# Phase 2 by token tiles of one batch with one stacked low-rank product; queries beside the chunks turned by VectorE

## The chip, the cores and the metric

The kernel runs on one core of one Trainium2 chip. The metric is the device time of one execution in microseconds (us). Before the change three executions took 1484.17, 1484.77 and 1485.76 us, so the median is 1484.77 us. The execution that the profiler recorded took 1491.34 us, and its first to last instruction spans 1489.6 us.

## The reference, cut to what matters

All arrays are float32, batch 8, 8 heads, 576 tokens, head size 64, model size 512.

```python
# attention through 32 packed queries per head
p_packed = sm_attn(p, k, v)              # (8, 8, 32, 64)
x = sm_attn(q, p_packed, p_packed)       # (8, 8, 576, 64) -> (8, 576, 512)
# first mixer (phase 1)
xk = mu_k * x + (1 - mu_k) * x_prev;  xr = mu_r * x + (1 - mu_r) * x_prev
x = sigmoid(xr @ w_r) * (relu(xk @ w_k) ** 2 @ w_v)
# second mixer (phase 2)
h = x.transpose(0, 2, 1) @ U @ V         # U (576, 32), V (32, 576): over the tokens
u = x + h.transpose(0, 2, 1)
out = u + relu(u @ w_ch1) @ w_ch2        # 512 -> 2048 -> 512
```

## The kernel before, in words

**Order of the work.** `Plan` collects every operation with its reads and writes, and `emit` lays the operations out on the engines with a list scheduler: it knows a cost for each operation, takes the ready operation of the lowest class first, on PE and SP in the order of the program and on the others in the order of becoming ready, and so fixes one instruction order for each engine and for SP's queue of DMA issues. On the chip each engine runs its list in order; an instruction that waits holds all behind it.

**Attention.** A unit is one pair of batches and one pair of heads; there are 16. Units 0 to 7 (`plain`) run ahead of everything else in several lanes. Units 8 to 15 run in one lane, A0, beside the chunks of phase 1; they are not plain. `attention_steps` (L648) does one unit: it turns k by TensorE, scores the packed queries, takes a softmax, turns q, forms the packed values `pp`, scores q against them and writes the result to `x_d`. For q it loads `qin` (`load_q`, L621): two DMAs, one for each batch, the tokens of the two batches in alternating partitions, runs of 64 floats. Then nine 128x128 transposes on TensorE, three into each PSUM bank (L718 to L731), and three copies of 384 columns, by ScalarE or VectorE, move the result to `qt`. In a unit of the lane A0 the next unit's q is loaded one unit ahead, as soon as its buffer is free: eight buffers of the pool `big` go round, eight to a unit. The scores for units 8 to 15 are turned back by VectorE (`turn`, L825 and L831).

**Phase 1** works on 12 chunks of 384 columns (`chunks`, three for each pair of batches); a column tile of 128 holds 64 tokens of each of the two batches. `mix` makes xk and xr, `r_block`, `k_block` and `v_block` do the three products with every fp32 operand split in a high and a low fp32r part, three products each (`PASS`). `x2_out` writes the rows of token tile i to `x2_d`, and `xu_block` sums x times U over the tokens and writes it to `xu_d` for each pair b of batches: rows for high and low part, batch and rank.

**Phase 2** works on 36 token tiles T of 128 tokens, nine for each pair of batches, four to a group q (`NQ` = 9). Tile T holds tokens 9p+i of both batches, 64 partitions each. `load_u` (L1252) loads it with one DMA. `h_block` (L1260) adds the low-rank term: two matmuls of 128x512 accumulate in one bank, with `vst` (the high part of V, then the low part, zero where the batch is the other one) as the stationary operand and `X` of the pair as the moving one; VectorE adds the bank to the tile. `load_xu` (L1240) makes `X` from four DMAs, one sum, one copy and one subtraction. `t_block` turns the tile for the next products, `operands` and `product` (L1319) run a seven-product scheme for u @ w_ch1, `c2_block` (L1342) multiplies by w_ch2 and, at a group's end, adds u and stores each tile by one DMA. The weights of `product` are streamed by DMAs that GpSimd issues (L319, `wb<-ws_d`). For each group the preparation of the next one (loads, `h_block`, `t_block`, `operands`) is spread over the eight steps f (L1487).

Of the kernel before, what the change touches and what calls it, by code (L numbers as in the profile page):

```python
# [9 lines left out]
F32 = mybir.dt.float32  # L10
F32R = mybir.dt.float32r
# [466 lines left out]
def packed_attention_moe_mixer_kernel(  # L478
# [36 lines left out]
    NPLAIN = 8  # L515
# [4 lines left out]
    plan = Plan(nc)  # L520
    add, sub, mul = ALU.add, ALU.subtract, ALU.mult
# [15 lines left out]
    x2_d = [dtile(f"x2_d{b}", [P, NI * DM], tuple(range(NI))) for b in range(NBP)]  # L537
    xu_d = [dtile(f"xu_d{b}", [P, DM]) for b in range(NBP)]
# [38 lines left out]
    class Bufs:  # L577
# [22 lines left out]
            return self.kept[1:]  # L600

        def tile_in(self, tag):
            return plan.tile(self.big_p, [P, 1152], F32, "big", parts=(0, 1, 2, 3), name=tag)

        def load_k(self, u, after=()):
            bp, j = divmod(u, NJ)
# [14 lines left out]
        def load_q(self, u, after=()):  # L621
            bp, j = divmod(u, NJ)
            if u not in self.qin:
                self.qin[u] = self.tile_in("qin")
            t = self.qin[u]
            for b2 in range(2):
                plan.dma(
                    t.at(b2)[b2:P:2, :].rearrange("p (i h d) -> p i h d", i=NI, h=2),
                    q[2 * bp + b2, 2 * j:2 * j + 2].rearrange("h (p i) d -> p i h d", i=NI), after=after)
# [18 lines left out]
    def attention_steps(A, u, u_next):  # L648
        bp, j = divmod(u, NJ)
        kin, qin, vin = A.kin.pop(u), A.qin.pop(u), A.vin.pop(u)  # L650
# [15 lines left out]
        for b2 in range(2):  # L666
            yield
            ps = ps_att()
# [5 lines left out]
        ps = ps_att()  # L674
# [36 lines left out]
        for b2 in range(2):  # L711
            r = slice(b2 * 64, (b2 + 1) * 64)
# [2 lines left out]
        plan.reduce(s0[:, 8:9], s1[:, 4:8], add)  # L715
        plan.recip(s0[:, 9:10], s0[:, 8:9])

        for c in range(3):  # L718
            yield
            ps = ps_att()  # L720
            for t in range(3):
                i = 3 * c + t
                plan.transpose(ps[:, t * P:(t + 1) * P], qin[:, i * P:(i + 1) * P], ident)
            n = 3 if c < 2 or not plain else 2
            w = 8 if plain else NI
            plan.copy(
                qt[:, 0:w * P].rearrange("p (b i c) -> p i b c", b=2, i=w)[:, 3 * c:3 * c + n],
                ps[:, 0:n * P].rearrange("p (i c b) -> p i b c", i=n, b=2))
            if c == 2 and plain:
# [11 lines left out]
        ps = ps_att()  # L741
# [4 lines left out]
        ps = ps_att()  # L746
        for t in range(5):
            for g in range(4):
# [4 lines left out]
                        start=(t == 0), stop=(t == 4), skip_group_check=True)  # L753
# [3 lines left out]
        if not plain:  # L757
            for b2 in range(2):
                r = slice(b2 * 64, (b2 + 1) * 64)
# [5 lines left out]
        ps = ps_att()  # L765
# [13 lines left out]
        if plain:  # L779
# [15 lines left out]
            for g, src, g0, g1 in ((0, psa, 0, 16), (1, psb[:, 0:P], 16, 20)):  # L795
                sv = src.rearrange("p (g k) -> p g k", k=NP)
# [8 lines left out]
            ps = ps_att()  # L805
# [4 lines left out]
            ps = ps_att()  # L810
# [4 lines left out]
        else:  # L815
            n = S // NP
# [371 lines left out]
    vst_ = []  # L1188

    def make_v():  # L1190
        vst = plan.tile(vx_p, [P, 2, NI, 2, 64], F32R, "vst", parts=(0, 1))
        vst_.append(vst)
        for c in range(2):
            raw = plan.tile(st_p, [P, 512], F32, "s", parts=(0, 1, 2, 3), name="raw_v")
            for g in range(4):
                plan.dma(raw.at(g)[g * 32:(g + 1) * 32, 0:288], v_d[:, c * 288:(c + 1) * 288])
            for i0, i1 in ((0, 5), (5, NI)):
                s = plan.tile(st_p, [P, 512], F32, "s", name="s_v")
                sv = s[:, 0:(i1 - i0) * 64].rearrange("p (i b c) -> p i b c", b=2, c=32)
                plan.zero(sv)  # L1200
                for g in range(4):
                    gr = slice(g * 32, (g + 1) * 32)
                    plan.copy(sv[gr, :, g % 2, :],
                              raw[gr, 0:288].rearrange("p (c i) -> p i c", i=NI)[:, i0:i1], ("dve",))
                sl = slice(c * 32, (c + 1) * 32)
                split(vst.at(0)[:, 0, i0:i1, :, sl], vst.at(1)[:, 1, i0:i1, :, sl], sv)

    def make_ws(f):
        r = []
# [28 lines left out]
        w2[m] = b  # L1238

    def load_xu(b):  # L1240
        xa = plan.tile(st_p, [P, 512], F32, "s", parts=(0, 1), name="xa")
        xb = plan.tile(st_p, [P, 512], F32, "s", parts=(0, 1), name="xb")
# [3 lines left out]
        plan.tt(xa[:, 0:512], xa[:, 0:512], xb[:, 0:512], add)  # L1246
        X = plan.tile(vx_p, [P, 512], F32R, "X")
        plan.copy(X, xa[:, 0:512])
        plan.tt(X[64:128, :], xa[64:128, 0:512], X[64:128, :], sub)
        xt[b] = X  # L1250

    def load_u(T):  # L1252
        b, i = divmod(T, NI)
        pl, tag = (((u_p, "u"),) * 4 + ((r_p, "r"),) * 3 + ((x2_p, "x2"),) * 3)[T % 10]
        u_t[T] = plan.tile(pl, [P, DM], F32, tag, name="u")
        plan.dma(u_t[T], x2_d[b].at(i)[:, i * DM:(i + 1) * DM])

    prep_banks = [ps_a]

    def h_block(T):  # L1260
        b, i = divmod(T, NI)
# [80 lines left out]
    def c2_block(q, m, th, h, last):  # L1342
        if (q, th) not in first:
            first.add((q, th))
            acc[q, th] = [plan.bank(ps_c2, "psc2") for _ in range(2)]
            fresh = True
        else:
            fresh = False
        w = w2[m]
        for t in range(2):  # L1350
            for i, (a, wi) in enumerate(PASS):
                plan.mm(acc[q, th][t], half(h, a)[:, t * P:(t + 1) * P], half(w, wi),
                        start=(fresh and i == 0), stop=(last and i == 2))
        if last:
            for t in range(2):
                T = 4 * q + 2 * th + t
                b, i = divmod(T, NI)
# [209 lines left out]
```

## Time and profile before

| | |
|---|---|
| median of three executions | 1484.77 us |
| profiled execution | 1491.34 us, span 1489.6 us |
| PE (TensorE matmul) busy | 1461.4 us, 98% of the span |
| PEld (weight load) | 1277.7 us, 86% |
| DVE (VectorE) | 980.2 us, 66% |
| ACT (ScalarE) | 728.3 us, 49% |
| POOL (GpSimd) | 270.3 us, 18% |
| mean granted TensorE clock | 0.983 of full speed |

Busy shares are means over stages with different limits, so each stage has to be read by itself. Up to about 130 us the first eight attention units run alone; then come the chunks of phase 1, up to about 520 us with attention beside them; from about 730 us it is phase 2. Matmuls are pipelined: the duration of one matmul is longer than its pitch, the time from its start to the start of the next, and the price of one in a full queue is the pitch. A line such as L197 is that of a helper that records every matmul, so groups are told apart by their tiles: `psat` is attention, `psk`, `psv`, `psr` are phase 1, `psh` is the low-rank term, `psc` the products of phase 2.

### The profile page before, as it was taken

How to read it: one execution, taken by the hardware profiler on the slowest of the kernel's cores; microseconds unless marked ns; L12 is line 12 of the kernel's file. 1: busy time of each engine (PE TensorE's matmuls, PEld its weight loads, DVE VectorE, ACT ScalarE, POOL GpSimd, SP SyncE). 2: the span in 40 equal slices, each digit the busy share in tenths (PEclk: the TensorE clock that was granted, in tenths of full speed). 3: DMA queues.
4: the chain of work that ended last, by engine and by line, in shares of the span. 5: the costliest groups of instructions: out<-in, count | busy, mean ns of one | idle time of the engine just before them, and what ended most of it. 6: DMA issues, size and time to landing. Idle time of an engine off the chain costs nothing.

```text
span 1489.6 us, 25587 instructions
## 1 busy us (share of the span) xinstructions
PE 1461.4 (98%) x9208; PEld 1277.7 (86%) x9208; DVE 980.2 (66%) x2143; ACT 728.3 (49%) x1534; POOL 270.3 (18%) x522
## 2 busy tenths in 40 slices
PE   6999999999999999999999999999999999999998
PEld 5667888888888888889899999899999999999997
DVE  6677877788888888786855464545555555554533
ACT  5567656666666666676533233323333332333332
POOL 0000000000000000001333333333333333333331
PEclk9689999999999999999999999999999999999999
DMA  8863335654655446666988888888888878878763
GB/s 233 234 175 121 114 101 137 205 182 136 186 179 156 141 141 218 207 226 191 314 228 237 211 208 245 198 244 229 231 212 229 213 201 239 213 216 222 206 176 99
DMA packets 213708, 292.42 MB, mean 196 GB/s; under 512 B 70224, under 2 KB 105360, under 8 KB 213584
## 3 DMA queue, kind: packets, MB, share of 16 engines
q1 hardware_dynamic: 141008, 158.65, 34.7%
q0 software_dynamic: 72576, 132.15, 34.0%
q8 instruction: 74, 1.21, 0.3%
q14 instruction: 50, 0.41, 0.1%
HBM read 229.84 MB, written 60.89 MB: 195 GB/s over the span
## 4 chain that ended last, share of the span: by engine, by line
PE 92%; DMA 3%; DVE 2%; SPq 1%; ACT 1%; issue 1%; DVEq 0%
PE psc L197 50%; PE psk L197 13%; PE psv L197 12%; PE psr L197 7%; PE psat L197 5%; PE psat L209 3%; SPq L319 1%; PE psh L197 1%; PE psu L197 1%; DMA kin<-in_k_dram 1%; DMA s<-w_d 1%; DMA qin<-in_q_dram 0%; DMA x_d<-xo 0%; DMA prs<-x_d 0%; DVE ob L254 0%
## 5 line engine op out<-in xcount | busy, mean ns | idle before, releaser
L197 PE MATMUL psc<-w,hid 128*128 128x512 f32 x1728 | 420.7, 391 | 0.2 <-ACT xu L288 0.2
L197 PEld LDWEIGHTS psc<-ob,wb 128*128 128x128 f32 x3024 | 386.4, 191 | 15.1 <-ACT tmp L288 0.8
L197 PE MATMUL psc<-ob,wb 128*128 128x256 f32 x3024 | 391.1, 282 | 0.4 <-ACT tmp L288 0.4
L319 POOL DMA_DIRECT2D wb<-ws_d x504 | 267.3, 530 | 565.5 <-PE psc L197 436.9
L197 PEld LDWEIGHTS psc<-w,hid 128*128 128x128 f32 x1728 | 314.9, 188 | 60.7 <-DVE hid L273 0.7
L233 ACT ACTIVATE hid<-tmp 128x256 fp32r<-128x256 f32 x216 | 131.6, 676 | 229.8 <-DVE tmp L254 229.8
L197 PE MATMUL psk<-xk,wk 128*128 128x384 f32 x1056 | 208.4, 340 | 1.3 <-ACT sq L233 0.8
L197 PE MATMUL psv<-wv,kk 128*128 128x512 f32 x783 | 202.0, 395 | 0.0
L197 PEld LDWEIGHTS psk<-xk,wk 128*128 128x128 f32 x1056 | 184.6, 188 | 10.6 <-issue 1.5
L197 PEld LDWEIGHTS psv<-wv,kk 128*128 128x128 f32 x783 | 144.2, 188 | 28.3 <-issue 0.8
L273 DVE SCALAR_TENSOR_TENSOR hid<-tmp,hid 128x256 fp32r<-128x256 f32 x216 | 126.5, 631 | 49.8 <-ACT hid L233 48.3
L254 DVE TENSOR_TENSOR tmp<-tmp,psc 128x256 f32<-128x256 f32 x288 | 113.1, 410 | 64.4 <-PE psc L197 64.1
L273 DVE SCALAR_TENSOR_TENSOR hid<-psc,hid 128x256 fp32r<-128x256 f32 x72 | 45.3, 629 | 166.5 <-ACT hid L233 166.5
L233 ACT ACTIVATE hid<-psc 128x256 fp32r<-128x256 f32 x72 | 45.9, 637 | 147.9 <-PE psc L197 147.5
L197 PE MATMUL psr<-wr,xr 128*128 128x512 f32 x414 | 112.3, 404 | 0.1
L311 POOL MEMSET x<- 128x8 f32 x4 | 0.5, 113 | 538.4 <-DVE m L270 538.1
L197 PEld LDWEIGHTS psr<-wr,xr 128*128 128x128 f32 x414 | 75.8, 190 | 18.4 <-issue 3.2
L288 ACT ACTIVATE tmp<-psc 128x256 f32<-128x256 f32 x144 | 56.5, 392 | 54.1 <-PE psc L197 53.5
L233 ACT ACTIVATE sq<-psk 128x384 f32<-128x384 f32 x96 | 46.5, 490 | 66.0 <-PE psk L197 63.6
L254 DVE TENSOR_TENSOR kk<-sq,kk 128x384 fp32r<-128x384 f32 x87 | 47.8, 552 | 32.0 <-ACT kk L288 31.8
L270 DVE SCALAR_TENSOR_TENSOR m<-x,mu_t,m 128x384 f32<-128x384 f32 x88 | 51.6, 610 | 0.9 <-ACT m L233 0.9
L233 ACT ACTIVATE m<-x,om_t 128x384 f32<-128x384 f32 x88 | 50.8, 607 | 2.5 <-DVE xr L254 1.8
(176 smaller groups left out, 1645.9 us busy)
## 6 DMA issues: line engine op xcount, KB each, us to landing
wb<-ws_d POOLq DMA_DIRECT2D x504, 256.0 KB, 3.7
st<-in_moe_w_ch_dram SPq DMA_DIRECT2D x32, 512.0 KB, 5.3
ws_d<-wb SPq DMA_DIRECT2D x56, 256.0 KB, 3.0
qin<-in_q_dram SPq DMA_DIRECT2D x32, 288.0 KB, 5.7
x_d<-xo SPq DMA_DIRECT2D x16, 576.0 KB, 3.4
x_d<-x SPq DMA_DIRECT2D x36, 256.0 KB, 2.2
u<-x_d SPq DMA_DIRECT2D x36, 256.0 KB, 5.2
out_dram<-u SPq DMA_DIRECT2D x36, 256.0 KB, 3.2
```

The lines of the kernel that those rows point to most:

```text
L197: self.nc.tensor.matmul(o, l, r, start=start, stop=stop, **k)
L209: self.nc.tensor.transpose(out.get(), in_.get(), ident.get())
L233: self.nc.scalar.activation(o, in_.get(), func, **k)
L254: return self.elem(engs, lambda e, o, x, y: e.tensor_tensor(out=o, in0=x, in1=y, op=op), out, [a, b], self.TT, cls)
L270: ("dve",), lambda e, o, x, y, z: e.scalar_tensor_tensor(out=o, in0=x, scalar=z, in1=y, op0=op0, op1=op1), out, [a, b, s], {"dve": (1.042, ...
L273: ("dve",), lambda e, o, x, y: e.scalar_tensor_tensor(out=o, in0=x, scalar=s, in1=y, op0=op0, op1=op1), out, [a, b], self.TT, cls)
L288: self.nc.scalar.activation(o, i, AF.Copy)
L311: (self.nc.gpsimd if eng == "pool" else self.nc.vector).memset(o, 0.0)
L319: (self.nc.sync if eng == "sp" else self.nc.gpsimd).dma_start(out=o, in_=i)
```

## The change

The diff, cut to its core:

```diff
@@ load_q
+            if u >= NPLAIN:
+                for b2 in range(2):
+                    for h in range(2):
+                        src = q[2 * bp + b2, 2 * j + h].rearrange("(r t) (e s) -> e r t s", t=2 * NI, e=2)
+                        for e in range(2):
+                            g = 2 * h + e
+                            plan.dma(t.at(2 * g + b2)[g * 32:(g + 1) * 32, b2 * S:(b2 + 1) * S]
+                                     .rearrange("p (t s) -> p t s", s=32), src[e], after=after)
+                return
@@ attention_steps
-        for c in range(3):
+        for c in range(3 if plain else 0):
...
+        if not plain:
+            yield
+            for b2 in range(2):
+                r = slice(b2 * S, (b2 + 1) * S)
+                plan.turn(qt[:, r].rearrange("p (i r e) -> p e i r", i=NI, e=2), qin[:, r])
@@ make_v
-        vst = plan.tile(vx_p, [P, 2, NI, 2, 64], F32R, "vst", parts=(0, 1))
+        vst = plan.tile(vx_p, [P, 12, 64], F32R, "vst")
+        plan.zero(vst[:, NI:NI + 2].bitcast(F32))
...
-            for i0, i1 in ((0, 5), (5, NI)):
...
-                plan.zero(sv)
-                for g in range(4):
...
-                split(vst.at(0)[:, 0, i0:i1, :, sl], vst.at(1)[:, 1, i0:i1, :, sl], sv)
+            rv = raw[:, 0:288].rearrange("p (c i) -> p i c", i=NI)
+            to = vst[:, 0:NI, c * 32:(c + 1) * 32]
+            plan.copy(to, rv, ("dve",))
+            for g in (1, 3):
+                gr = slice(g * 32, (g + 1) * 32)
+                plan.tt(to[gr], rv[gr], to[gr], sub)
+        plan.copy(vst[:, NI + 2], vst[:, NI - 1], ("dve",))
@@ load_xu
-        for d in range(2):
-            plan.dma(xa.at(d)[d * 64:(d + 1) * 64, 0:512], xu_d[b][0:64, :])
-            plan.dma(xb.at(d)[d * 64:(d + 1) * 64, 0:512], xu_d[b][64:128, :])
...
+        for b2 in range(2):
+            xa = plan.tile(st_p, [P, 512], F32, "s", parts=(0, 1, 2, 3), name="xa")
+            xb = plan.tile(st_p, [P, 512], F32, "s", parts=(0, 1, 2, 3), name="xb")
+            for g in range(4):
+                for a, t in ((0, xa), (1, xb)):
+                    r = a * 64 + b2 * NP
+                    plan.dma(t.at(g)[g * 32:(g + 1) * 32, :], xu_d[b][r:r + NP, :])
+            plan.tt(xa, xa, xb, add)
+            X = plan.tile(vx_p, [P, 512], F32R, f"X{b2}")
+            plan.copy(X, xa)
+            plan.tt(X[64:128, :], xa[64:128], X[64:128, :], sub)
+            xt[b, b2] = X
@@ new; load_u, h_block and c2_block use it
+    def halves_of(T):
+        b, t = divmod(T, NI)
+        if t == NI - 1:
+            return b, [(slice(0, P), t, slice(0, P))]
+        b2, k2 = divmod(t, 4)
+        return b, [(slice(e * 64, (e + 1) * 64), 2 * k2 + e, slice(b2 * 64, (b2 + 1) * 64)) for e in range(2)]
@@ load_u
-        plan.dma(u_t[T], x2_d[b].at(i)[:, i * DM:(i + 1) * DM])
+        for n, (to, i, rows) in enumerate(hs):
+            t = u_t[T].at(n) if len(hs) > 1 else u_t[T]
+            plan.dma(t[to], x2_d[b].at(i)[rows, i * DM:(i + 1) * DM])
@@ h_block
-        for a in range(2):
-            plan.mm(ps, vst_[0].at(a)[:, a, i].rearrange("p b c -> p (b c)"), xt[b], start=(a == 0), stop=(a == 1))
+        if t < NI - 1:
+            k2 = t % 4
+            plan.mm(ps, vst_[0][:, 2 * k2:2 * k2 + 2].rearrange("p e c -> p (e c)"), xt[b, t // 4],
+                    start=True, stop=True)
+        else:
+            for b2 in range(2):
+                plan.mm(ps, vst_[0][:, NI - 1 + 2 * b2:NI + 1 + 2 * b2].rearrange("p e c -> p (e c)"), xt[b, b2],
+                        start=(b2 == 0), stop=(b2 == 1))
@@ c2_block, at a group's end
-                plan.dma(dst[:, i, :], u)
+                for to, i, rows in hs:
+                    plan.dma(dst[rows, i, :], u[to])
```

For units 8 to 15 q is loaded by eight DMAs of 32 partitions with runs of 32 floats, so that each batch lies in its own 576 columns, and two 32x32-block transposes on VectorE make `qt`, 128x576 each; the nine TensorE transposes and three copies of such a unit are gone. Buffers of `big` have eight parts, for the dependencies of the eight DMAs.

In phase 2 the first eight tiles of a pair of batches hold 128 tokens of one batch each (two blocks of 64 rows of `x2_d`); the ninth holds what is left of both. `vst` and `X` stack high and low parts in the four groups of 32 partitions, with `X` for each batch apart (`X0`, `X1`), so that one matmul over 128 partitions gives all four high and low products; the ninth tile takes two. Such tiles are loaded and stored by two DMAs of 64 partitions.

## Rows read from the trace of the kernel before

**Rows 1.** Page, part 2: tenths of busy time, and granted clock, in 40 slices.
```profile
PE   6999999999999999999999999999999999999998
PEclk9689999999999999999999999999999999999999
```
**Rows 2.** Windows: attention beside chunks, phase 2; PE, PEld, DVE, ACT, POOL busy; clock, DMA.
```profile
150.00:520.00 370.00, 367.26 (x2375) 314.68 (x2374) 306.85 (x677) 247.89 (x522) 0.23 (x2) 1.00 0.50 153
750.00:1450.00 700.00, 700.00 (x4367) 632.90 (x4366) 376.05 (x781) 231.66 (x442) 241.29 (x456) 1.00 0.82 219
```
**Rows 3.** Waits: waiter, line, releaser: us in all, times, longest.
```profile
PE psat L209 <- DMA kin<-in_k_dram: 8.7, 5, 3.6
...
PE psc L197 <- ACT tmp L288: 0.4, 1, 0.4
...
ACT ob L288 <- DMA ut<-uq_d: 21.0, 8, 3.4
```
**Rows 4.** Timeline of PE in phase 2: start, us until the last ends, group, count.
```profile
1361.37 2.91 PE L197 MATMUL psc<-w,hid 128*128 128x512 f32 x12
...
1364.83 0.63 PE L197 MATMUL psh<-X,vst 128*128 128x512 f32 x2
1365.30 2.30 PE L197 MATMUL psc<-ob,wb 128*128 128x256 f32 x18
```
**Rows 5.** Tile psh: the low-rank matmuls, ns min/median/max, first and last start.
```profile
L197 PE MATMUL psh<-X,vst x72: 387/396/403, 671.8 to 1365.1; 128*128 128x512 f32 x72
```
**Rows 6.** Timeline of PE between two bursts of one unit's q transposes.
```profile
315.87 0.49 PE L209 MATMUL psat<-ident,qin 128*128 128x128 f32 x3
316.12 0.95 PE L197 MATMUL psr<-wr,xr 128*128 128x512 f32 x3
316.90 0.49 PE L209 MATMUL psat<-ident,qin 128*128 128x128 f32 x3
```
**Rows 7.** Groups by form in 150 to 520 us: q's copies, VectorE's turns.
```profile
L288 ACT ACTIVATE qt<-psat 128x384 f32<-128x384 f32 x15 | 7.3, 491 | 4.4 <-PE psat L209 4.2
...
L215 DVE STREAM_TRANSPOSE qt<-a 128x576 f32<-128x576 f32 x8 | 6.2, 772 | 0.0
...
L291 DVE COPY qt<-psat 128x384 f32<-128x384 f32 x9 | 5.0, 555 | 4.2 <-PE psat L209 4.2
```
**Rows 8.** Tile u: SP's load issues, strided turns; ns min/median/max, first and last start.
```profile
L319 SPq DMA_DIRECT2D u<-x_d x36: 319/327/1414, 571.3 to 1321.0; - x36
...
L215 DVE STREAM_TRANSPOSE ux<-u x32: 677/690/712, 725.9 to 1366.7; 128x512 f32<-128x512 f32 x32
```
**Rows 9.** Tile qin: SP's issues of its DMAs, and the landing.
```profile
L319 SPq DMA_DIRECT2D qin<-in_q_dram x32: 602/736/2368, 4.5 to 459.2; - x32
...
DMA to landing us min/median/max: 3.9/5.7/9.2
```
**Rows 10.** Timelines: q loads on SP, of unit 8 and a later one; unit 8's transposes.
```profile
221.95 1.40 SPq L319 DMA_DIRECT2D qin<-in_q_dram  x2
...
275.29 1.70 SPq L319 DMA_DIRECT2D qin<-in_q_dram  x2
...
239.59 0.49 PE L209 MATMUL psat<-ident,qin 128*128 128x128 f32 x3
```
**Rows 11.** Tile xa: its loads, and the subtraction that ends X.
```profile
L319 SPq DMA_DIRECT2D xa<-xu_d x8: 450/540/596, 632.6 to 981.3; - x8
...
L254 DVE TENSOR_TENSOR X<-xa,X x4: 689/690/691, 640.1 to 1183.4; 64x512 fp32r<-64x512 f32 x4
```
**Rows 12.** Timeline of the end: the last group's four sums on VectorE.
```profile
1483.64 2.58 DVE L254 TENSOR_TENSOR u<-psc,u 128x512 f32<-128x512 f32 x4 [0.59 <-PE psc L197]
```
**Rows 13.** DMA issues: loads of k; KB each, median us from issue to landing.
```profile
kin<-in_k_dram SPq DMA_DIRECT2D x32, 256.0 KB, 4.4
```
**Rows 14.** Timelines: chunk 6's last x loads on SP, and the first mix after them.
```profile
389.96 1.50 SPq L319 DMA_DIRECT2D x<-x_d  x2
...
412.34 0.61 ACT L233 ACTIVATE m<-x,om_t 128x384 f32<-128x384 f32 x1
```

More of the change, by code (lines that the diff above doesn't have):

```diff
@@ L602, in tile_in @@
         def tile_in(self, tag):
-            return plan.tile(self.big_p, [P, 1152], F32, "big", parts=(0, 1, 2, 3), name=tag)
+            return plan.tile(self.big_p, [P, 1152], F32, "big", parts=tuple(range(8)), name=tag)
         def load_k(self, u, after=()):
@@ L723, in attention_steps @@
                 plan.transpose(ps[:, t * P:(t + 1) * P], qin[:, i * P:(i + 1) * P], ident)
-            n = 3 if c < 2 or not plain else 2
-            w = 8 if plain else NI
+            n = 3 if c < 2 else 2
             plan.copy(
-                qt[:, 0:w * P].rearrange("p (b i c) -> p i b c", b=2, i=w)[:, 3 * c:3 * c + n],
+                qt[:, 0:8 * P].rearrange("p (b i c) -> p i b c", b=2, i=8)[:, 3 * c:3 * c + n],
                 ps[:, 0:n * P].rearrange("p (i c b) -> p i b c", i=n, b=2))
-            if c == 2 and plain:
+            if c == 2:
                 plan.copy(qt[:, 1024:1152].rearrange("p (b c) -> p b c", b=2),
                           ps[:, 2 * P:3 * P].rearrange("p (c b) -> p b c", b=2))
+        if not plain:
[3 more added lines that the diff above has]
+                plan.turn(qt[:, r].rearrange("p (i r e) -> p e i r", i=NI, e=2), qin[:, r])
         if early:
@@ L1196, in make_v @@
                 plan.dma(raw.at(g)[g * 32:(g + 1) * 32, 0:288], v_d[:, c * 288:(c + 1) * 288])
-            for i0, i1 in ((0, 5), (5, NI)):
-                s = plan.tile(st_p, [P, 512], F32, "s", name="s_v")
-                sv = s[:, 0:(i1 - i0) * 64].rearrange("p (i b c) -> p i b c", b=2, c=32)
-                plan.zero(sv)
-                for g in range(4):
[L1202 to L1205, printed above, removed]
-                split(vst.at(0)[:, 0, i0:i1, :, sl], vst.at(1)[:, 1, i0:i1, :, sl], sv)
+            rv = raw[:, 0:288].rearrange("p (c i) -> p i c", i=NI)
[5 more added lines that the diff above has]
+        plan.copy(vst[:, NI + 2], vst[:, NI - 1], ("dve",))
     def make_ws(f):
@@ L1240, in load_xu @@
     def load_xu(b):
-        xa = plan.tile(st_p, [P, 512], F32, "s", parts=(0, 1), name="xa")
-        xb = plan.tile(st_p, [P, 512], F32, "s", parts=(0, 1), name="xb")
-        for d in range(2):
-            plan.dma(xa.at(d)[d * 64:(d + 1) * 64, 0:512], xu_d[b][0:64, :])
-            plan.dma(xb.at(d)[d * 64:(d + 1) * 64, 0:512], xu_d[b][64:128, :])
-        plan.tt(xa[:, 0:512], xa[:, 0:512], xb[:, 0:512], add)
-        X = plan.tile(vx_p, [P, 512], F32R, "X")
-        plan.copy(X, xa[:, 0:512])
@@ L1249, in load_xu @@
-        plan.tt(X[64:128, :], xa[64:128, 0:512], X[64:128, :], sub)
-        xt[b] = X
+        for b2 in range(2):
[10 more added lines that the diff above has]
+            xt[b, b2] = X
@@ L1252, in load_u @@
+    def halves_of(T):
[4 more added lines that the diff above has]
+        return b, [(slice(e * 64, (e + 1) * 64), 2 * k2 + e, slice(b2 * 64, (b2 + 1) * 64)) for e in range(2)]
     def load_u(T):
-        b, i = divmod(T, NI)
+        b, hs = halves_of(T)
         pl, tag = (((u_p, "u"),) * 4 + ((r_p, "r"),) * 3 + ((x2_p, "x2"),) * 3)[T % 10]
-        u_t[T] = plan.tile(pl, [P, DM], F32, tag, name="u")
@@ L1256, in load_u @@
-        plan.dma(u_t[T], x2_d[b].at(i)[:, i * DM:(i + 1) * DM])
+        u_t[T] = plan.tile(pl, [P, DM], F32, tag, name="u", parts=(0, 1))
+        for n, (to, i, rows) in enumerate(hs):
+            t = u_t[T].at(n) if len(hs) > 1 else u_t[T]
+            plan.dma(t[to], x2_d[b].at(i)[rows, i * DM:(i + 1) * DM])
     prep_banks = [ps_a]
     def h_block(T):
-        b, i = divmod(T, NI)
+        b, t = divmod(T, NI)
         ps = plan.bank(prep_banks[0], "psh")
-        for a in range(2):
-            plan.mm(ps, vst_[0].at(a)[:, a, i].rearrange("p b c -> p (b c)"), xt[b], start=(a == 0), stop=(a == 1))
+        if t < NI - 1:
[6 more added lines that the diff above has]
+                        start=(b2 == 0), stop=(b2 == 1))
@@ L1356, in c2_block @@
                 T = 4 * q + 2 * th + t
-                b, i = divmod(T, NI)
+                b, hs = halves_of(T)
                 u = u_t.pop(T)
```

## The prediction

> **What bounds the kernel now.** I read the page's busy slices first [rows 1]: TensorE (PE) is at nine tenths or more in every slice but the first and the last, and the granted clock is at full (2.4 GHz) but for dips in the first slices, where attention runs alone; the change leaves that stretch as it is. Then the windows of the two stages that it does touch [rows 2]. Beside the chunks PE is busy 367.3 of 370 us, with VectorE (DVE) next at 306.9 (83%) and ScalarE (ACT) at 247.9. In phase 2 PE is busy 700.0 of 700, DVE 376.1, and the DMA engines 0.82 of the time. A busy PE need not be a bound PE, so the waits come next [rows 3]: PE's longest wait in total is 8.7 us for loads of k; on the products of phase 2 the largest is a single one of 0.4 us. Last the timeline of PE [rows 4]: twelve 512-column matmuls take 2.91 us, so with 0.39 us for the last one the pitch is (2.91 - 0.39) / 11 = 0.229 us, and the next group starts before the last has ended. The order of PE is one queue without holes from about 150 us to the end, so a matmul that is taken out is worth its pitch, unless something else then comes late.
>
> **The change part by part.** All sums are made against the profiled execution of 1491.3 us (span 1489.6 us and 1.7 us around it); it lies 6.6 us above the median of 1484.8 us. I carry the difference in us over to the median; scaling it by 1484.8 / 1491.3 would change it by under 0.1 us.
>
> *Low-rank product.* Before there are 72 matmuls for 36 tiles [rows 5]. After, a pair of batches takes 8 x 1 + 2 = 10, so 40; 32 go. The two of rows 4 start at 1364.83 and what follows at 1365.30, so one costs 0.47 / 2 = 0.235 us. 32 x 0.235 = 7.5 us off PE.
>
> *Transposes of q.* Nine in each of 8 units, 72 in all, go. Within a burst the pitch is (0.49 - 0.27) / 2 = 0.11 us. From burst to burst [rows 6] 1.03 us hold three transposes and three 512-column matmuls; less 3 x 0.229 that leaves 0.114 us each, with the switch between kinds in it. 72 x 0.11 to 0.114 = 7.9 to 8.2 us; I take 8.0. Together 15.5 us off PE.
>
> *Copies and turns.* In these units 24 copies of 384 columns go: 9 from DVE (5.0 us) and 15 from ACT (7.3 us) [rows 7]. Sixteen turns of 128x576 come, all on DVE; the trace has that form at 772 ns, and a turn that writes every second element, as the new one does, at 690 ns for 512 columns [rows 8], which is no dearer per column. 16 x 0.772 = 12.4 us, so DVE gets 7.4 us more and ACT 7.3 us less. DVE in that stage goes from 306.9 of 370 (83%) to 314.3 of 362 (87%). The cover is the 48 us that DVE still has idle there. Behind a turn in DVE's queue stand the chunk's mixes and splits, for which PE's next products wait; two turns hold them 1.5 us at most. Bounds: if PE had to pay for all of DVE's growth, +7.4 us; if the eight units' shorter chain (no bank, no copy between load and `qt`) closed every hole that PE has there, -2.7 us (370 - 367.3). I take +1.0, near no effect, since PE has 2.7 us of holes now with DVE already at 83%.
>
> *Loads of q.* Eight DMAs in place of two, and twice as many packets of half the size. The issue of one is bounded by 0.33 us (a load of 128 packets [rows 8]) and 0.74 us (1152 packets of 256 bytes [rows 9]); eight take 2.6 to 5.9 us of SP's queue, against 1.5 now, so 1.1 to 4.4 more for each unit. Behind them in the queue stand v, the next k and x. For landing I bound by 5.7 us as now for 288 KB and by twice that for each 288 KB. The turn waits for all eight. The load stands a unit ahead: one unit's is issued at 275.3 [rows 10] and its transposes are under way at 315.9 [rows 6]; even 5.9 + 11.4 = 17.3 us fit in 40. Unit 8 alone is tight: issued at 221.95, used at 239.59, 17.6 us. The planner may put its turn earlier on DVE, as it no longer waits for a PSUM bank, and so before the data are there; I count 0 to 5 us of DVE wait once, and nothing of it for PE.
>
> *Making X and V.* Each pair of batches has 16 loads in place of 4, at 0.54 us of SP [rows 11] 6.5 us more, and two sums, copies and subtractions in place of one: about 1.4 us more of DVE by the 0.69 us of such an operation. For the first pair, X is ready at 641 and first used at 671.8 [rows 5, 11], so 8 us more are hidden; the others' loads are issued long before use. In phase 2 DVE is busy 376 of 700 us, and ACT already waits up to 3.4 us for `ut`, eight times, with PE late 0.4 us in all [rows 2, 3]. V's copies shrink. Cost 0; without that cover 4 x 2 = 8 us.
>
> *Halved loads and stores of u.* 32 more loads and 32 more stores at 0.33 us of SP each [rows 8], the same packets of 2 KB and the same bytes. SP is not full there. At the very end the four sums come 0.65 us apart (2.58 / 4) [rows 12] and three of the four stores become two issues of 0.33 us: they fit; 0 to 0.3 us, I take 0.
>
> Sum: -7.5 - 8.0 + 1.0 = -14.5 us: 1476.8 us for the profiled execution, **1470.3 us** for the median. Bounds: -15.5 - 2.7 = -18.2 (1466.6) and -15.5 + 7.4 = -8.1 (1476.7).
>
> One rule of the Trainium skill speaks against taking PE at its busy time. [...] The pitch of rows 4 and the missing waits of rows 3 disagree, so I keep the full saving and give the rule's figure 10 of the forecast's 65%; it lies in the same range.
>
> **The rivals.**
> *A, DVE becomes the bound beside the chunks.* For it: DVE at 83%, in long in-order chains (mix, split, split of kk) that PE needs; turns sit in front of them. Against: ACT loses 7.3 us and the planner can give it copies, and PE's holes are 2.7 us in 370 with DVE as full as it is. Then nothing of the 8.0 us arrives and only phase 2 pays: 1484.8 - 7.5 = 1477.3 us.
> *B, slower: SP's queue of issues.* Six more issues for each q stand before v, k and x in one in-order queue. The place is where chunk 6's x comes in among attention's loads [rows 14]: its last loads go out at 390.0 to 391.5, and the mix that follows starts at 412.3, so about 18 us of cover with some 3 us of landing. If that cover is gone and each unit exposes its 1.1 to 4.4 us, 8 units cost 9 to 35 us: 1478 to 1504 us, with 1490 in the middle; it is slower than before from 1.9 us for each unit (15.5 / 8). Against: k and v are loaded a unit ahead too, and six issues in some 40 us of a unit are little of SP's time. The Trainium skill adds to this rival: DMA: Bandwidth & Descriptors, "Specifications", wants at least 512 bytes a transfer, since below it the engine reads before it writes. The rows show little of that so far: 288 KB of q in 256-byte runs land in 5.7 us, 256 KB of k in runs of mostly 1 KB in 4.4 [rows 9, 13], 15% more for each KB.
> *C, a larger gain.* PE's holes beside the chunks close as 24 trips through PSUM go: -18.2 us, 1466.6 us, and some more if the chunks' own waits shrink.
> *D, no change:* the saved work is replaced by waits that the planner's order did not foresee, around 1484 us.
>
> **How the numbers follow.** Forecast 65%, A 13%, C 8%, B 8%, D 6%. 0.2% is 3 us, about what can be told from no change here. Forecast, A and C are faster by more, 0.86; D is within it, 0.06; B is slower, 0.08, the little of B on either side of the bound left out. The range takes in the forecast with its bounds, most of A and part of C: 1466 to 1478 us; outside are D, B and the far end of C.
>
> **What would show it.** In the changed profile `psh` has 40 matmuls at the same pitch; `qin` appears in transposes of TensorE only in the first eight units; 16 turns of about 0.77 us stand on DVE. PE stays at nine tenths in all slices, phase 2 is shorter by about 7 us and the stretch up to it by about 7. Wrong would be: new waits of PE for DVE's splits between 220 and 520 us (A), waits for `vin`, `kin` or the chunks' x on DMA (B), turns of over 0.9 us, or a lower granted clock after 150 us.

## The result and the profile after

The changed kernel takes **1505.61 us** (median of 6 runs, 1500.64 to 1507.09); the kernel before took 1487.01 us beside it (6 runs, 1484.17 to 1492.78). The ratio is 1.0121 [1.01, 1.0141]: 18 us slower, where 14.5 us faster was predicted. The profiled execution took 1506.06 us, with a span of 1504.3 us.

The page of the changed kernel, part 2, answers to [rows 1]:

```profile
PE   6999999999999999998599999999999999999998
...
PEclk8799999999999999999799999999999999999999
```

There is a hole in the nineteenth and twentieth slice, at the border between the chunks and phase 2, which before did not have. The windows of that stretch show it, first of the kernel before, then of the changed one (columns as in [rows 2]):

```profile
700.00:750.00 50.00, 49.43 (x295) 43.53 (x294) 37.97 (x75) 27.01 (x53) 14.31 (x27) 1.00 0.89 268
```
```profile
650.00:700.00 50.00, 50.00 (x251) 44.19 (x250) 40.96 (x97) 34.16 (x79) 2.25 (x4) 1.00 0.61 205
700.00:750.00 50.00, 29.66 (x138) 22.63 (x137) 30.26 (x56) 17.97 (x33) 10.59 (x21) 0.76 1.10 307
```

PE idles 20 us there (50 less 29.66), and the granted clock falls to a mean of 0.76. Read in windows of 5 us, it is 0.50 from 715 to 725 and from 735 to 740, the lower of its two levels (1.2 GHz), and PE had been waiting ahead of both pieces. The changed kernel's waits (as [rows 3]) name new entries under the old one for k:

```profile
PE psat L209 <- DMA kin<-in_k_dram: 10.3, 5, 3.9
PE psc L197 <- ACT hid L233: 9.8, 1, 9.8
PE psh L197 <- DVE u L254: 6.4, 4, 2.5
PE psc L197 <- ACT w L288: 2.8, 1, 2.8
```

**Marks.** To see what each stage took I set five marks in each trace: the first `psr` on PE (end of the lead, in which attention runs alone; in the trace before it comes at 91.7 us, ahead of the 130 us given above), the last store of x2 (`x_d<-x`, end of the chunks), the first store of `out`, the first store of the last group, and the end of the span. The rows, of the tiles `psr`, `w_d`, `ws_d`, `x_d` and `out_dram`, with first and last start in the last two numbers ahead of the semicolon; before:

```profile
L197 PE MATMUL psr<-wr,xr x414: 387/389/793, 91.7 to 671.6; 128*128 128x512 f32 x138
...
L319 SPq DMA_DIRECT2D w_d<-m x32: 319/333/546, 271.1 to 570.9; - x32
...
L319 SPq DMA_DIRECT2D ws_d<-wb x56: 319/367/1072, 584.5 to 687.3; - x56
...
L319 SPq DMA_DIRECT2D x_d<-x x36: 319/320/1900, 215.2 to 714.3; - x36
...
L319 SPq DMA_DIRECT2D out_dram<-u x36: 332/333/1227, 800.0 to 1486.3; - x36
```

and after:

```profile
L197 PE MATMUL psr<-wr,xr x414: 387/389/505, 90.1 to 663.6; 128*128 128x512 f32 x138
...
L319 SPq DMA_DIRECT2D w_d<-m x32: 319/341/1087, 272.8 to 586.8; - x32
...
L319 SPq DMA_DIRECT2D ws_d<-wb x56: 319/372/1743, 598.5 to 721.5; - x56
...
L319 SPq DMA_DIRECT2D x_d<-x x36: 319/332/1267, 212.0 to 704.7; - x36
...
L319 SPq DMA_DIRECT2D out_dram<-u x68: 357/578/759, 817.8 to 1500.8; - x68
```

The chunks took 714.3 - 91.7 = 622.6 us before and 704.7 - 90.1 = 614.6 after. But `w_d` (the casts: the weights of w_ch1, w_ch2 and V, split into parts by background work) ends at 586.8 in place of 570.9, and `ws_d` (the second weights that `make_ws` sums from them for phase 2) at 721.5 in place of 687.3. Before it ended 27.0 us ahead of the last x2 store, after 16.8 us behind it. From the last x2 store to the first store of `out` it takes 85.7 us before, 113.1 after.

The runs by these marks, from one profiled execution each, in us ("ahead": last `ws_d` store to last x2 store; "sum": stage + border + groups + tail against 1397.9 before; "ratio": all timed runs):

| run | chunks | ahead | border | eight groups | tail | sum | ratio to before [95%] |
|---|---|---|---|---|---|---|---|
| before | 622.6 | 27 | 85.7 | 684.4 | 5.2 | 0 | 1 |
| after | 614.6 | -17 | 113.1 | 679.2 | 7.3 | +16.3 | 1.0121 [1.01, 1.0141] |
| e1 attention part | 615.5 | -17 | 107.0 | 684.1 | 5.2 | +13.9 | 1.0078 [1.0063, 1.0093] |
| e2 phase 2 part | 622.0 | 32 | 88.7 | 681.1 | 7.3 | +1.2 | 1.0027 [1.0012, 1.0042] |
| e3 change, GpSimd helps | 624.5 | 31 | 90.3 | 680.5 | 7.3 | +4.7 | 1.0048 [1.0029, 1.0066] |
| e4 before, GpSimd helps | 628.2 | 52 | 86.9 | 684.0 | 5.6 | +6.8 | 1.0047 [1.0033, 1.0061] |
| e6 before + turns | 622.5 | 27 | 86.0 | 684.8 | 5.2 | +0.6 | 1.0003 [0.9991, 1.0014] |
| e7 attention part, ACT | 613.4 | -13 | 106.6 | 684.8 | 5.2 | +12.1 | 1.007 [1.005, 1.009] |
| e8 change, casts' class | 618.9 | 31 | 90.9 | 680.3 | 7.3 | -0.5 | 0.9985 [0.9973, 0.9998] |
| e9 before, half DMAs | 624.1 | 35 | 86.2 | 685.1 | 7.8 | +5.3 | 1.0036 [1.0021, 1.0051] |
| e10 change, order, GpSimd stores | 618.6 | 35 | 92.7 | 680.6 | 9.7 | +3.7 | 1.0009 [0.9993, 1.0025] |
| e11 before, order | 625.5 | 30 | 86.0 | 684.5 | 5.2 | +3.3 | 1.0021 [1.0006, 1.0036] |
| e12 change, order | 617.3 | 35 | 90.0 | 681.5 | 7.3 | -1.8 | 0.9995 [0.9982, 1.0008] |
| e17 phase 2, interleaved | 622.8 | 26 | 88.7 | 679.7 | 5.6 | -1.1 | 1.0011 [0.9997, 1.0025] |
| e18 change, order, interleaved | 618.8 | 31 | 88.1 | 679.2 | 5.6 | -6.2 | 0.9967 [0.9954, 0.9981] |

e5 has no row, because its profiled execution fell in a slow state (1787.03 us, granted clock 0.748) and only its other times are used. e13 to e16, which are over 15% slower, have none either. The lead is left out of the sums: it is the same code in all runs and took 84 to 92 us from one execution to the next. Sum and ratio differ by up to 2.8 us, since the marks come from a single execution; those of e2 and e17 come from the fastest of their twelve.

By these marks gains of the size that was forecast are there, 8.0 us beside the chunks and 5.2 in the groups, and 27.4 us were lost at the border and 2.1 in the tail. Work that is put off from the chunks to the border would shorten the first and lengthen the second; e8, e11 and e12 below bear on how much of the 8.0 us is such work.

**How the hole comes about.** SP's timeline of the changed kernel around the end of the chunks:

```profile
688.64 1.05 SPq L319 DMA_DIRECT2D raw<-w_d  x2
689.81 10.08 SPq L319 DMA_DIRECT2D ws_d<-wb  x9
...
706.04 3.51 SPq L319 DMA_DIRECT2D u<-x_d  x5
...
717.61 0.42 SPq L319 DMA_DIRECT2D s<-w_d  x1
718.14 0.72 SPq L319 DMA_DIRECT2D ws_d<-wb  x1
...
721.51 0.46 SPq L319 DMA_DIRECT2D ws_d<-wb  x1
```

`make_ws` is still storing when the chunks are over, and w2's loads (`s<-w_d`; w2 is w_ch2 for `c2_block`), which share the buffers `s` with it, start at 717.6, 12.9 us behind the last x2 store. Before, the first of them stood 30.9 us ahead of that store:

```profile
683.41 0.38 SPq L319 DMA_DIRECT2D s<-w_d  x1
```

PE's timeline of the changed kernel shows what follows (in brackets the idle time before the row and its releaser):

```profile
712.29 0.50 PE L197 MATMUL psh<-X,vst 128*128 128x512 f32 x1 [2.54 <-DVE u L254]
...
721.96 5.13 PE L197 MATMUL psc<-w,hid 128*128 128x512 f32 x12 [2.84 <-ACT w L288]
...
738.99 1.65 PE L197 MATMUL psc<-w,hid 128*128 128x512 f32 x3 [9.75 <-ACT hid L233]
```

PE's wait that ends at 721.96 is for w2: ScalarE's first part of its split had waited 6.6 us for the load. The one of 9.75 us is for `hid`, and what `hid` needs stands in VectorE's queue behind more splits of w2 and behind `ob`, which waited 5.3 us for the turned u (`ut<-uq_d`). The twelve matmuls at 721.96 take 5.13 us where [rows 4] have 2.91 for twelve; the granted clock there is 0.50.

### The profile page after: what moved, and what is told of

Its sections match the earlier page's. It is cut to its first block, busy times and chain, and to the rows that moved or that the text cites. A ratio compares the mean times of both kernels' runs of the same rounds, so it can differ in the third digit from the quotient of the medians.

```text
span 1504.3 us, 25595 instructions
## 1 busy us (share of the span) xinstructions
PE 1450.2 (96%) x9104; PEld 1264.2 (84%) x9104; DVE 984.2 (65%) x2131; ACT 720.9 (48%) x1531; POOL 268.6 (18%) x519
## 4 chain that ended last, share of the span: by engine, by line
PE 88%; DMA 4%; DVE 3%; ACT 2%; SPq 2%; issue 1%; DVEq 0%; ACTq 0%
PE psc L197 50%; PE psk L197 12%; PE psv L197 11%; PE psr L197 7%; PE psat L197 4%; PE psat L209 2%; SPq L319 2%; DMA kin<-in_k_dram 1%; DMA u<-x_d 1%; PE psu L197 1%; PE psh L197 1%; DMA s<-w_d 1%; ACT a L233 0%; DMA st<-in_moe_w_v_dram 0%; DMA st<-in_moe_w_ch_dram 0%
## 5 line engine op out<-in xcount | busy, mean ns | idle before, releaser
L197 PE MATMUL psr<-wr,xr 128*128 128x512 f32 x414 | 108.9, 399 | 0.2
L254 DVE TENSOR_TENSOR ob<-ut,ob 128x512 fp32r<-128x512 f32 x45 | 30.8, 688 | 36.3 <-ACT ob L288 36.3
```

Source lines behind the costliest of these rows:

```text
L197: self.nc.tensor.matmul(o, l, r, start=start, stop=stop, **k)
L254: return self.elem(engs, lambda e, o, x, y: e.tensor_tensor(out=o, in0=x, in1=y, op=op), out, [a, b], self.TT, cls)
```

## The experiments

**Which part.** e1 is the kernel before with the change's `load_q`, `tile_in` and q part of `attention_steps` alone; e2 has all the rest of the change and not these.

> The changed kernel's attention part alone (eight loads and two VectorE turns for q in units 8 to 15); phase 2 as before. Before is 1487, the change 1505.6 us. Theory 1 (starved background: the turns and the faster attention take VectorE's spare time from the work of the lowest class, the casts of phase 2's weights and the making of their sums, so the gap at the stage border appears): 1500 to 1513 us, with a hole of PE of over 15 us at the border and the casts' last store later than before's 570.9 us. Theory 2 (SP: six more issues of q's loads a unit hold up what stands behind them): also slow, 1500 or more, since the issues are in this part; not told apart here. Theory 3 (phase 2's part: sixteen X loads and four buffers of the shared ring of five delay the border): 1479 us, no hole.

> The changed kernel's phase 2 part alone (one stacked product for a tile of one batch, halved loads and stores, X for each batch apart); attention as before. Theories 1 and 2: PE saves 32 x 0.235 = 7.5 us and nothing starves: 1478 to 1483 us against 1487. Theory 3: the hole at the border is here: 1500 us or more.

Measured: e1 1498.11 us, e2 1491.53. The hole belongs to the attention part (border 107.0, `ws_d` 17 us behind the last x2 store); the phase 2 part does not have it, but gains nothing, where 1478 to 1483 us was expected.

**Does VectorE lack the time for the casts?** e3 (on the change) and e4 (on before) give the casts' sums and `make_ws`'s splits to GpSimd:

```diff
-                plan.tt(m, m, a, add)
+                plan.tt(m, m, a, add, ("pool",))
...
-            split(half(bl[i], 0), half(bl[i], 1), src)
+            split(half(bl[i], 0), half(bl[i], 1), src, ("pool",))
```

> The change, with two of the background's operations moved from VectorE to GpSimd, which is idle until phase 2: the last addition of each of the 32 casts (512 columns, 0.68 us on VectorE) and the subtractions of the splits of phase 2's first weights (56 of 256 columns, 0.42 us each), together some 45 us off VectorE. SP's issues and phase 2 stay those of the change. Theory 1: the casts and the weights are ready in time, the hole at the border closes, and PE's saving arrives: 1466 to 1475 us. Theory 2: nothing of SP's queue is changed, so 1500 us or more. Theory 3: 1495 or more, since X's loads and the ring stay.

> The kernel before with the same two operations on GpSimd. Theory 1: before, the background was ready in time, so there is little to win: 1480 to 1488 us, and what e3 wins is not just GpSimd's help. If the gain is GpSimd's whatever the change, this one is faster by the same 30 us or so as e3 is than the change, 1455 us.

Measured: 1491.74 and 1493.97 us, both slower than expected. The hole closes in e3 (`ws_d` 31 us ahead, border 90.3), which ties the border to the background work. But the chunks get 9.9 us longer on the change and 5.6 us longer on before, so e3 still stays behind the kernel before.

**What in the attention part?** e5 gives before the eight short-run DMAs of q (runs of 32 floats, half the former length) and nothing else; e6 adds to before the 16 turns into `qt`, whose result the old copies then overwrite; e7 is e1 with each turn replaced by a ScalarE copy, which leaves the 32x32 blocks unturned.

```diff
 e6, ahead of the nine transposes
+        if not plain:
+            for b2 in range(2):
+                r = slice(b2 * S, (b2 + 1) * S)
+                plan.turn(qt[:, r].rearrange("p (i r e) -> p e i r", i=NI, e=2), qin[:, r])
 e7
-                plan.turn(qt[:, r].rearrange("p (i r e) -> p e i r", i=NI, e=2), qin[:, r])
+                plan.copy(qt[:, r].rearrange(...), qin[:, r].rearrange("p (e i r) -> p e i r", e=2, i=NI), ("act",))
```

> The kernel before with q of units 8 to 15 loaded by eight DMAs in runs of 32 floats (as many DMAs, packets and bytes as in the change, in the layout of before); nothing else is changed. Theory 2 (SP's issues and short packets hold up the loads of the casts and so the border): the casts end 10 us or more later than before's 570.9 us and the time is 1495 us or more. Theory 1 (VectorE's spare time): 1483 to 1488 us, as before, and the casts end within 5 us of before.

> The kernel before with the two turns of q on VectorE added in units 8 to 15; their result is written over by the transposes and copies that stay, so this adds 12.4 us of VectorE and nothing else. Theory 1: the casts end later, by 5 to 20 us (12.4 us taken from work of the lowest class), while the stage beside the chunks keeps its length; weights for phase 2 were ready 27 us ahead of the border, so the time rises by 5 us at most: 1485 to 1491 us. Theory 2: the casts end as before, 1485 us.

> e1 (the attention part alone) with each turn of VectorE replaced by a copy on ScalarE of the same 128x576 elements, so q is not turned within its blocks of 32 and the output differs; loads, SP's issues and TensorE are those of e1. Theory 1: VectorE has 12.4 us more for the background, the casts end earlier against the stage's end than in e1 (119 us ahead of the last store of phase 1's output; before 143), the gap from there to the first output store shrinks from 107 us towards 90, and the time is 1480 to 1490 us. Theory 2: as e1, 1498 us.

Measured: e5 0.9987 [0.9975, 1.0], e6 1.0003 [0.9991, 1.0014], e7 1.007 [1.005, 1.009]. On the kernel before, as many short DMAs cost nothing (each over 64 alternate partitions, where the change has 32), and neither do 16 more turns on VectorE; e7 has no turns on VectorE, and the hole is still there. The `ws_d` rows of e6, then of e7:

```profile
L319 SPq DMA_DIRECT2D ws_d<-wb x56: 319/370/1412, 579.9 to 680.0; - x56
```
```profile
L319 SPq DMA_DIRECT2D ws_d<-wb x56: 319/320/1984, 593.6 to 711.3; - x56
```

What these runs leave is the order that the planner writes when q's transposes and copies are gone.

**Is it the order?** e8 is the change with one line: the casts from chunk 7 on go from class 3, which the planner takes last, to class 1, that of the chunks.

```diff
-            plan.cls = 3
+            plan.cls = 3 if n < 7 else 1
```

> The change with one edit of the planner's order: the casts that are planned at chunks 7 and 8 get class 1, that of the chunks' own work, in place of 3. No operation is added, removed or moved to another engine. Theory 1: these casts are no longer left for last, the weights of phase 2 are ready before the border, the gap falls from 113 us to 85 to 92 and the time is 1472 to 1483 us, faster than before. Theory 2: SP issues the same DMAs, so the border stays late: 1497 us or more.

Measured: 1483.29 us, 22 us less than the changed kernel (20 by the two ratios, 17 by the marks). Its `ws_d` row and its window, to be read against those of the changed kernel above:

```profile
L319 SPq DMA_DIRECT2D ws_d<-wb x56: 319/369/861, 573.9 to 671.3; - x56
```
```profile
700.00:750.00 50.00, 45.15 (x257) 39.51 (x257) 30.82 (x63) 20.03 (x38) 14.84 (x28) 0.93 1.13 280
```

So the cause of most of the border's loss is shown: late background work, set by its class in the planner. Of the 27.4 us 22.2 go (border 90.9), and e2 has 3.0 of the rest. VectorE had the time for the casts: from 520 to 600 us it is busy 66.7 of 80 us before, 58.8 in the changed kernel and 68.0 in e8, with PE full in all three (79.5 to 80.0). e8 keeps q's DMAs and turns. Of the 8.0 us beside the chunks 4.3 are given back (618.9); with one and the same order on both kernels (e11 and e12 below) the change has 8.2 us less there.

**The halved DMAs.** e9 is the kernel before with every u load and every out store cut in two of 64 partitions.

```diff
-        plan.dma(u_t[T], x2_d[b].at(i)[:, i * DM:(i + 1) * DM])
+        for e in range(2):
+            r = slice(e * 64, (e + 1) * 64)
+            plan.dma(u_t[T].at(e)[r], x2_d[b].at(i)[r, i * DM:(i + 1) * DM])
...
-                plan.dma(dst[:, i, :], u)
+                for e in range(2):
+                    r = slice(e * 64, (e + 1) * 64)
+                    plan.dma(dst[r, i, :], u[r])
```

> The kernel before, with every load of u and every store of out cut into two DMAs of 64 partitions each; bytes, packets and work are the same. Theory (halved transfers are what ate the low-rank product's gain): the tail after the last group grows from 5.2 to about 7.3 us, the stage border by 2 to 3 us and the groups by 0 to 1, so 3 to 6 us slower than before, a ratio of 1.002 to 1.004, and an issue on SP at 0.58 us in place of 0.33. Rival (the prediction's term): halved issues fit into SP's idle time, 0 to 0.3 us, a ratio of 0.9995 to 1.0005.

Measured: 1491.03 us, 5.3 us slower by its ratio and by its marks, 2.6 of them in the tail. The end of the changed kernel shows why: SP's row, VectorE's row (as [rows 12]) and the DMA engines in forty slices of 1494 to 1504 us:

```profile
1497.02 4.29 SPq L319 DMA_DIRECT2D out_dram<-u  x7
```
```profile
1496.30 2.58 DVE L254 TENSOR_TENSOR u<-psc,u 128x512 f32<-128x512 f32 x4 [0.59 <-PE psc L197]
```
```profile
DMA  0000000000000000398988999899979899800000
GB/s 0 0 0 0 0 0 0 0 0 0 0 0 0 0 0 0 90 229 180 246 172 205 205 205 246 164 205 213 221 180 221 164 344 385 320 0 0 0 0 0
```

VectorE is done at 1498.88, but SP issues until 1501.3 and the engines, nine tenths busy, move about 205 GB/s; only the whole store at the end gets up to 385, as all four did before (336 to 401 in slices of 0.25 us). SP's issues alone, 0.6 us for 128 KB, would give about the same rate, so the packets have to decide: from 1470 us on the last four tiles' stores, 1.05 MB in both, take 2.8 us of each DMA engine before and 4.9 us in e9 (2.8 again in e18 below, whose stores span 128 partitions). So the transfers themselves take longer. The Trainium skill has this: SBUF — State Buffer, "Door 1: The DMA port swizzle (why `[64,N]` ≈ `[32,N]`)", says that partitions 0 to 63 reach no more than 8 of 16 ports, as do 64 to 127, and gives 196 GB/s measured for 64 in transfers of 1 MiB; the trace agrees with its 205.

**Order, and stores by GpSimd.** e12 changes more classes: attention's last four units go from 0 to 1, so they no longer come first, and the casts from chunk 5 on from 3 to 1. e10 is e12 with the second halves of the last group's stores issued by GpSimd, e11 has e12's two lines on before.

> The changed kernel with the planner's class for attention's last four units set from 0 to 1, for the casts from chunk 5 on from 3 to 1, and in the last group the second halves of the stores issued by GpSimd. Theory (the gain beside the chunks, 8 us, and in the groups, 5 us, is there and was lost at the border and the tail): the last store of the second weights comes 20 us or more ahead of the last x2 store, the border takes 86 to 91 us in place of 113, the tail 5.5 to 6.5 us; sum 10 to 14 us faster than before, 1472 to 1478 us. Rival (the casts moved earlier take PE's or VectorE's time from the chunks): the stage beside the chunks gets 5 us longer or more and the total stays at the 1483 us of the run that only raised the late casts' class.

> The kernel before with the same two classes changed (attention's last four units from 0 to 1, the casts from chunk 5 on from 3 to 1) and nothing else. Theory: before has no hole at the border for these classes to close, its last store of the second weights being 27 us ahead of the last x2 store; so within 3 us of before, a ratio of 0.998 to 1.002. Rival (the order by itself is the gain): 6 us or more faster, a ratio under 0.996.

> The changed kernel with the two classes changed and all stores left to SP. Theory: 1 to 2 us slower than the run with GpSimd's stores, from the tail alone (7.3 us in place of 5.5 to 6.5); 1474 to 1479 us. Rival (the tail is set by the DMA engines, not by SP's issues): the same tail, and the two runs within 0.5 us.

Measured: 1487.24 us, ratio 1.0009 [0.9993, 1.0025]; 1488.2; 1485.24. The expected 10 to 14 us did not come: e12 stays 4.3 us over before at the border and 2.1 in the tail, and GpSimd's issues make the tail longer (9.7 us in e10), not shorter. On before the order costs 3 us, so it is no gain by itself. e2 has as much in the tail (2.1) and 3.0 at the border, so I looked at the phase 2 part next.

**Whole DMAs, first attempt.** e13 takes the phase 2 part, e14 the change, e15 and e16 the change with e8's and e12's order, each with one DMA for a tile of u; the DRAM side then has two outer steps of 64 rows.

```diff
-                for to, i, rows in hs:
-                    plan.dma(dst[rows, i, :], u[to])
+                plan.dma(dst[rows, i:i + n, :].rearrange("p e f -> e p f"), u)
```

> The phase 2 part alone on the kernel before (one product for two token tiles, X and V made its way), but each tile of u loaded by one DMA and stored by one, of 128 partitions, in place of two of 64. Theory (the halved transfers cost 5.3 us, as they did on the kernel before, and hide the low-rank gain): tail 5.2 us, border 84 to 86, groups 84.9 to 85.1; 4 to 7.5 us faster than before, a ratio of 0.995 to 0.997, against 1.0027 with halves. Rival (the product's 32 matmuls are not worth their pitch): ratio 0.999 to 1.001.

Measured: 1721.75 us, ratio 1.1583 [1.1555, 1.1612]; e14 to e16, which were expected at ratios of 0.9925 to 1.010, have 1.1542 to 1.1634. All missed by far. The DMA engines in 1703 to 1709 us, in e13's tail of 19.9 us:

```profile
DMA  0120101111111101111111011111110111111111
GB/s 27 55 27 0 55 27 27 41 55 41 55 55 55 55 27 55 55 55 55 55 55 55 27 55 55 55 55 55 55 55 27 55 55 55 55 55 55 41 41 55
```

One tenth busy, about 50 GB/s: an eighth of 385, as if two of sixteen engines worked. That is what the Trainium skill says (DMA: Bandwidth & Descriptors, "Why a DMA increments its semaphore by 16 and not by 1"): a DMA runs on the largest number of engines up to 16 that divides the slowest dimension of both sides, here two.

**Whole DMAs, second attempt.** In e17 (phase 2 part) and e18 (change with e12's order) the two token tiles alternate over the partitions, 2c + e in place of 64e + c, and V's stack has its columns in that order; one DMA then has 128 partitions and 64 outer rows of 4 KB.

```diff
-                for to, i, rows in hs:
-                    plan.dma(dst[rows, i, :], u[to])
+                plan.dma(dst[rows, i:i + n, :], u)
... load_u likewise; make_v writes the columns as
+  vst[:, 0:8].rearrange("p (k e) c -> p k (e c)", k=4).rearrange("p k (c e) -> p k c e", e=2)
```

> The phase 2 part alone on the kernel before, with the tokens of a tile of u interleaved over the partitions (the columns of V's stack in the same order), so that each tile is one DMA of 128 partitions with 64 outer rows of 4 KB in DRAM, for load and store. Theory (halves hid the low-rank gain): tail 5.2 us, border 84 to 86, groups 84.9 to 85.1; 4 to 7.5 us faster than before, a ratio of 0.995 to 0.997. Rival (the product's 32 matmuls are not worth their pitch): 0.999 to 1.001. If 64 outer rows are as slow for the DMA engines as 64 partitions were: tail 7 us and 1.001 to 1.004, as with the halves.

> The whole change with the tokens of a tile of u interleaved over the partitions and whole DMAs, attention's last four units and the casts from chunk 5 on in class 1. Theory: stage beside the chunks 617 us from the lead's end, border 86 to 88, groups 85.0, tail 5.2: 7 to 11 us faster than before, a ratio of 0.9925 to 0.9955. Rival (what the casts' order costs beside the chunks and the border's loads eat it): 0.998 to 1.000.

Measured: e17 1487.93 us, e18 **1480.69 us**, ratio 0.9967 [0.9954, 0.9981]: faster than both kernels, by 0.33% against before, which is clear of its interval but less than expected (0.9925 to 0.9955). e17's engines at the end, 1472 to 1482 us, are back at the full rate, and the tail is 5.6 us:

```profile
DMA  0000000000000000000000899999999992000000
GB/s 0 0 0 0 0 0 0 0 0 0 0 0 0 0 0 0 0 0 0 0 0 0 311 385 377 344 369 393 369 401 385 377 393 90 0 0 0 0 0 0
```

e17's groups are 4.7 us shorter than before's, so the low-rank saving is there; against it stands the border, 3.0 us longer, in an execution that was 4.2 us faster than e17's median. PE's waits from 695 to 800 us come to 4.0 us in e17 and to 0.6 before. The largest of them comes from VectorE. These rows show it there, then on PE, and then SP's queue with the loads behind it:

```profile
744.90 0.69 DVE L254 TENSOR_TENSOR xa<-xa,xb 128x512 f32<-128x512 f32 x1 [7.01 <-DMA xb<-xu_d]
...
746.44 0.59 DVE L273 SCALAR_TENSOR_TENSOR hid<-psc,hid 128x256 fp32r<-128x256 f32 x1
```
```profile
747.09 1.20 PE L197 MATMUL psc<-w,hid 128*128 128x512 f32 x4 [2.36 <-DVE hid L273]
```
```profile
729.05 1.93 SPq L319 DMA_DIRECT2D xa<-xu_d  x4
731.09 4.74 SPq L319 DMA_DIRECT2D ut<-uq_d  x4
736.45 1.71 SPq L319 DMA_DIRECT2D xb<-xu_d  x4
738.85 4.18 SPq L319 DMA_DIRECT2D xa<-xu_d  x4
```

The sum for an X stands in VectorE's in-order queue and waits 7.0 us for the loads of its two operands, eight DMAs; `hid` stands behind it, and PE waits 2.4 us for `hid`. The same chain stands in other runs with the phase 2 part (PE's wait is 2.4 us in e2 and e12, 1.9 in e8, 1.2 in e18); PE has no such wait in before, e6 or e9. No run took it away, so that it makes up the border's 3 us is read from the traces and not shown.

## Why the prediction was wrong

*Low-rank product, -7.5: right.* `psh` of the changed kernel (as [rows 5]) has the 40 matmuls, at the same duration:

```profile
L197 PE MATMUL psh<-X,vst x40: 389/396/794, 663.9 to 1377.7; 128*128 128x512 f32 x40
```

Of the 32 that went, 26 lay in the eight groups (56 before, 30 after), 26 x 0.235 = 6.1 us; the groups are 5.2 us shorter (5.2 in e18, 4.7 in e17).

*Transposes of q and VectorE's growth, -8.0 + 1.0: right in size.* The chunks are 8.0 us shorter (7.1 in e1, 8.2 between e11 and e12, which have the same order). The turns and q's issues are as priced (rows of tile `qin`, as [rows 9]):

```profile
L319 SPq DMA_DIRECT2D qin<-in_q_dram x80: 560/630/1767, 4.6 to 446.6; - x80
...
L215 DVE STREAM_TRANSPOSE qt<-qin x16: 756/772/776, 231.3 to 467.6; 128x576 f32<-128x576 f32 x16
```

Perfetto Trace Analysis in the Trainium skill ("Identifying the Most-Contended Engine") holds matmul busy time for no good measure of how near a kernel is to the chip's limit (its roofline), and names the share of weight loads as one that is. Taken as the part of the saving that counts, that share (85% in [rows 2]) would give 6.8 - 1.0 = 5.8 us, an estimate by that page, against the forecast's 7.0. The measured 7.1 to 8.2 lie nearer the forecast, but this stage takes from 622.0 to 624.1 us in runs that leave it alone (before, e2, e6, e9, e17), so 1.2 us are not told apart. No run here has q in runs over the 512 bytes of the prediction's other rule of the Trainium skill; e5 halved them from 256 to 128 bytes at a ratio of 0.9987.

*The step that failed* is the first part's conclusion, "a matmul that is taken out is worth its pitch, unless something else then comes late", with a sum that has no price for anything coming late at the border. PE's queue without holes says that all background work was ready in time, not by how much. The casts and second weights had a slack of 27 us at the border, visible in before's `ws_d` and `x_d` rows, and no step of the prediction read it. Counted from the end of the lead, the change ends the chunks 8.0 us earlier and, through the planner's order, the background 35.8 us later, and the border grows by 27.4 us. e8 shows it: one class moved, 22 us back. Which of the planner's choices delays the casts stays open; e6 and e7 speak against the turns' time on VectorE, e5 and e8 against the DMAs.

*Halved loads and stores, "0 to 0.3, I take 0": wrong by 5 us* on the kernel before (e9), and by some 4 us on the change (e18 against e12). The term counted issues of 0.33 us and equal packets. The issues of the halves take 0.58 (the changed kernel's row, as [rows 8]), and the transfer itself runs at about half the rate:

```profile
L319 SPq DMA_DIRECT2D u<-x_d x68: 325/588/849, 587.2 to 1336.2; - x68
```

*Making X and V, 0:* the cover named was X's readiness for its first use. Overlooked was who stands behind its sum in VectorE's queue; in e17 that goes with 2.4 us of PE's wait, between the 0 taken and the bound of 8.

*The rivals.* The range of B, 1478 to 1504, was near the time, but by luck: its mechanism, SP's issues of q, is not the cause (e5, and e8, which keeps them). A did not come (chunks 8.0 us shorter, 16 turns free in e6), nor C. D was the nearest in kind, waits in place of the saved work, but it named no place for them and priced them at the saving, 14.5 us, where the border alone took 27.4. Of the signs of being wrong one came, a lower granted clock after 150 us, as a result of the hole.

## What to carry to other kernels

Where a list scheduler fills a stage with work for the next one that it takes last, a saving in this stage is worth its size only if that work keeps its slack: look up when its last store comes against the stage's end, before summing pitches. When a tile comes to hold two halves, try interleaving them over the partitions before cutting the DMA: here one DMA over 128 partitions with 64 outer rows kept the full rate, and neither two of 64 partitions nor one with an outer dimension of 2 did.

## What the runs showed of the hardware

- Stores of 64 partitions moved about 205 GB/s with the DMA engines nine tenths busy (end of the changed kernel), those of 128 partitions up to 385 to 401 (before, e17).
- The issue of a tile of u on SP took 0.33 us for 128 partitions (before) and 0.58 for 64, but 0.55 to 0.57 for the interleaved DMA of 128 partitions in e17 too. So its length does not go by the partitions alone, and a slower issue did not keep e17's stores from the full rate.
- Stores whose DRAM side has an outer dimension of 2 moved about 50 GB/s, with the engines one tenth busy (e13).
- GpSimd's help beside the chunks makes them longer. In e4 VectorE runs fewer instructions but is busy for longer, 318.5 of 370 us against 306.9 in [rows 2]; several of the same operations take longer there (`a<-st,m`, 128x512: a mean of 820 ns against 683), and the sum that moved takes GpSimd 1471 ns where it took VectorE 679:

```profile
150.00:520.00 370.00, 367.41 (x2373) 314.18 (x2372) 318.46 (x657) 244.76 (x522) 42.37 (x32) 1.00 0.50 156
```
